# Identity products around a transpose, a scaling on VectorE, and later weight and query loads in a fused DeltaNet and maxout-FFN kernel

## The chip, the cores and the metric

The kernel runs on one core of one Trainium2 chip. The metric is device time in microseconds of one execution, and a kernel's time is the median of its runs. A core has five engines with queues of their own: PE (TensorE, matrix products), DVE (VectorE), ACT (ScalarE), POOL (GpSimd) and SP (SyncE, which only issues DMAs here). Each engine works its queue in program order, so an instruction that waits holds up all that stand behind it on its engine. PEld is the loading of PE's stationary operand.

## The reference

Queries, keys and values are 4 batches x 8 heads x 768 positions x 48. The first layer is a delta rule with a 48x48 state for each batch and head; the second is a maxout FFN over 3072 tokens of width 384, with hidden width 768.

```python
k_n = k / (np.linalg.norm(k, axis=-1, keepdims=True) + 1e-06)
for t in range(S):
    y[:, :, t] = einsum('bhd,bhde->bhe', q[:, :, t], state)
    v_old = einsum('bhde,bhd->bhe', state, k_n[:, :, t])
    state = state + beta[t] * einsum('bhd,bhe->bhde', k_n[:, :, t], v[:, :, t] - v_old)
x = y.transpose(0, 2, 1, 3).reshape(B * S, H * D)
h = maximum(maximum(x @ w1, x @ w2), x @ w3)
out = h @ w_out
```

## The kernel before, in words

**Chunks.** The 768 positions are cut into 12 chunks of 64. Two chunks make a group of 512 tokens, so there are six groups. Inside a chunk the recurrence is written with products: of keys with keys (the tile `at`), of keys with queries (`pt`), and with the inverse of a triangular matrix (`ut`), which is found by `solve(m)` for a whole group at once. `solve` is a generator: each `yield` is one elimination step, two VectorE operations (L561 and L565), and the main program takes steps with `some(solving, n)`. Group 0 is solved before the FFN starts, group 1 while the FFN of group 0 runs.

**One chunk's links.** For chunk c: `halves_z` (e) and `halves_u` (f) finish the second half of the inverse for chunk 1 (products p_e, p_f); `join_z` (z, p_z) and `join_u` (j, p_j) join the halves; `turn_t1` (d) transposes; `old_k` (k) subtracts p_k from v on VectorE at L755; `old_q` (q) is p_q; `new` (u) is p_u; `step` (s) adds p_s to the state `st` on VectorE at L801; `to_y` (y) is p_y; `to_x` (x) transposes y on PE (p_x, L832) and copies it to `xt` on ACT (L839). The FFN of the group reads `xt`.

**Other letters.** S is one solve step, M masks `pt`, T n is `turn(n, (1,))`, the transposes of query unit n with their copy, after which `load_q(n + 3)` is issued while n + 3 < 11; P is the product of keys and queries of a unit. A unit is half a chunk's batches: chunk c has the units 2c and 2c + 1. Query units take turns in three buffers (`qall`), values (`v_t`) in three.

**The FFN of group 0** (`ffn(0)`) yields after each hidden tile: i = 0, 1, 2 are the three maxout weights of the first 128 hidden columns for 256 tokens, and so on to i = 17; from i = 18 on they are 512 tokens wide; i = 27 to 30 are the outputs. Each of them is three products p_h (L1224; two records each) into one of two PSUM buffers, and a copy on ACT or a maximum on VectorE (L1238). The loop over i in the main program (L1452) writes out by hand what stands between two such tiles: the strings in `FIRST` (links, solve steps, turns), `EARLY_LINKS` (links of chunks 2 and 3), loads, fetches and conversions. The order of the text is the order on each engine.

**Weights.** The weights come as 24 pieces of 384 KB. `fetch(queue)` issues the DMA of the next one into one of five buffers (`w_bits`), and waits on its queue until that buffer is free. `some(conv, 1)` converts one piece: three ACT operations (L247 to L249), a VectorE shift (L259) and a GpSimd addition (L263), the last two one conversion late. Pieces 0 to 5 are fetched before the loop; pieces 9 to 17 are used from i = 18 on. The first four conversions stand before the loop, six at i = 0 to 5, and the rest from i = 11 on.

**Values.** `load_v(c)` issues two DMAs, and `scale(c, nrm)` (L295) multiplies the chunk's values by the norms of its keys, on GpSimd for chunks 0 to 9 and on VectorE after that. `prep_values(2)` is the scaling of chunk 2, at i = 8.

**Around the change.** The end of the part before the loop is, in the order of the text: the products p_u and p_y of chunk 0, the transposes of `halves_t(1)`, the start of `solve(1)` (norms, ACT's zeroing of its PSUM tile y_p at L525, L547), `to_x(0)`, one conversion. Then the loop starts with i = 0. `busy(n, of)` (L1290) issues n products of the identity with `of` into a PSUM tile p_w of the same two buffers as p_h; nothing reads it. It is called once before the change, with six products, at the very start.

Of the kernel before, what the change touches and what calls it, by code (L numbers as in the profile page):

```python
# [23 lines left out]
def kernel(  # L24
# [31 lines left out]
    nc = tc.nc  # L56
# [32 lines left out]
    def ps_ffn(shape, name):  # L89
        return psum.tile(shape, FP32, name=name, tag="ffn", bufs=2)  # L90

    def ps_two(name):
        return pairs.tile([128, 2, 512], FP32, name=name, tag="two", bufs=3)
# [7 lines left out]
    ident = const.tile([128, 128], FP32, name="ident")  # L101
# [16 lines left out]
    def rows(bb):  # L118
        return slice(C * bb, C * (bb + 1))
# [6 lines left out]
    def load(src, dst, n, queues):  # L126
        c, g = divmod(n, 2)
        for bb in range(2):
            queues[bb].dma_start(
                out=dst[rows(bb ^ g), :, 0:D],  # L130
                in_=src[2 * bb + g, :, c * C : (c + 1) * C, :].rearrange(
                    "h p d -> p h d"
                ),
            )
# [4 lines left out]
    def load_k(n, queues=one_queue):  # L139
        load(k, kpad[place(n)], n, queues)  # L140

    def load_q(n, queues=one_queue):
        load(q, qpad[n % NQ], n, queues)

    def load_v(c, queue=nc.sync):
        vts[c] = work.tile([128, 2, H, D], FP32, name="v_t", bufs=3)
        for bb in range(2):
            queue.dma_start(  # L148
                out=vts[c][rows(bb)].rearrange("p g h d -> p (g h) d"),
                in_=v[2 * bb : 2 * bb + 2, :, c * C : (c + 1) * C, :].rearrange(  # L150
                    "b h p d -> p (b h) d"
                ),
            )
# [66 lines left out]
    def fetch(queue=nc.scalar):  # L220
        if fetched[0] < len(pieces):
            _, src, (a, b) = pieces[fetched[0]]
            st = work.tile([128, 2 * 384], U32, name="w_bits", bufs=5)
            queue.dma_start(
                out=st.rearrange("p (a b) -> p a b", a=a), in_=src
            )
            staged.append(st)
            fetched[0] += 1
# [63 lines left out]
                )  # L292
            nrms[2 * m + cc] = t[:, 16:32].rearrange("p (g h) -> p g h", g=2)

    def scale(c, nrm):  # L295
        (nc.vector if c > 9 else nc.gpsimd).tensor_tensor(
            out=vts[c], in0=vts[c],
            in1=nrm[:, :, :, None].to_broadcast([128, 2, H, D]), op=ALU.mult,
        )

    def prep_values(c):

        if c in nrms:
            scale(c, nrms.pop(c))


    nrm_0 = const.tile([128, 2, 2, H], FP32, name="nrm_0")
# [179 lines left out]
    def blocks(m, queue=nc.sync):  # L487
        if m == 1:
            xs[m] = in_wo(0)
        else:  # L490
            xs[m] = work.tile([128, 2, HB * BL + HB], FP32, name="x_bl", bufs=1)
        queue.dma_start(
            out=in_rows(xs[m]),
            in_=at_d[m].rearrange("c f b h j i -> (c f b h) j i"),
        )
# [323 lines left out]
    def to_x(c):  # L819
        m, cc = divmod(c, 2)  # L820
        if m not in xts:
            xts[m] = work.tile([128, KT, TOK], FP32, name="xt")
        y_f = yts.pop(c).rearrange("p g h d -> p g (h d)")
        xt = xts[m][:, :, cc * 256 : (cc + 1) * 256].rearrange(
            "p t (g x) -> p g t x", g=2
        )
        p_x = ps_two("p_x")
        for g in range(2):
            if g and not c:
                p_x = ps_two("p_x")  # L830
            for t in range(KT):
                nc.tensor.transpose(  # L832
                    p_x[:, g, t * 128 : (t + 1) * 128],
                    y_f[:, g, t::KT],
                    ident,
                )
            of = p_x[:, :, 0 : KT * 128].rearrange("p g (t x) -> p g t x", t=KT)
            if not c:
                nc.scalar.copy(xt[:, g], of[:, g])  # L839
        if c:  # L840
            nc.scalar.copy(xt, of)
# [37 lines left out]
    def less_first(f):  # L879
        part = (slice(None), slice(None), slice(f * 128, (f + 1) * 128))  # L880
        for i in (1, 2):
            nc.vector.tensor_tensor(
                out=w_sb[i][part], in0=w_sb[i][part], in1=w_sb[0][part],
                op=ALU.subtract,
            )

    def turn_first(fs):
        p_f = ps_two("p_t")
        for i, f in enumerate(fs):
            for t in range(KT):  # L890
                nc.tensor.transpose(
                    p_f[:, i, t * 128 : (t + 1) * 128],
                    w_sb[0][:, t, f * 128 : (f + 1) * 128],
                    ident,
                )
        for i, f in enumerate(fs):
            nc.scalar.copy(
                w_sb[0][:, :, f * 128 : (f + 1) * 128],
                p_f[:, i, 0 : KT * 128].rearrange("p (t x) -> p t x", t=KT),
            )  # L900
# [375 lines left out]
    def some(gen, n):  # L1276
        for _ in range(n):
            if next(gen, gen) is gen:
                break
# [10 lines left out]
    def busy(n, of):  # L1290
        p_w = ps_ffn([128, TOK], "p_w")[:, 0 : of.shape[1]]
        for _ in range(n):
            nc.tensor.matmul(p_w, ident, of)
# [55 lines left out]
    some(conv, 1)  # L1349
    placed(1, 0)  # L1350
    scale(0, nrm_0[:, 0])
    placed(1, 1, nc.gpsimd.tensor_copy)
    blocks(1, nc.gpsimd)
    for _ in range(2):
# [16 lines left out]
    halves_t(1)  # L1371
    solving = solve(1)
    some(solving, 1)
    to_x(0)
    some(conv, 1)


# [28 lines left out]


    FIRST = {
        0: "e1 s0 S1 S1", 1: "f1 k1 S1 S1 S1", 2: "z1 d1 M2 S1 S1",
        3: "j1 S1 q1 M3 S1 S1", 4: "u1 T4", 5: "y1", 6: "s1 T5", 7: "x1 T6",  # L1410
        8: "T7", 14: "P4", 15: "P5", 21: "P6", 22: "P7",
    }

# [12 lines left out]
    def links(m, names):  # L1426
        for name in names.split():
            f, i = name[0], int(name[1])
            if f in RECURS and m < GROUPS:
                RECURS[f](2 * m + i)  # L1430
            elif f in MADE and m + 1 < GROUPS:
                MADE[f](2 * (m + 1) + i)
            elif f in UNIT and m + 1 < GROUPS:
                UNIT[f](4 * (m + 1) + i)
            elif f == "N" and m + 2 < GROUPS:
                load_blocks(4 * (m + 2) + i)

    def queries(names):
        for name in names.split():
            f, n = name[0], int(name[1])  # L1440
            if f not in OF_KEYS:
                links(0, name)
                continue
            OF_KEYS[f](n)
            if f == "T" and n + 3 < 11:
                load_q(n + 3)
# [3 lines left out]
    CONVERTED = {*range(6), *range(11, 25)}  # L1450
    FETCHED = {8: 1, 12: 1, 13: 1, 14: 1, 18: 2, 19: 2, 20: 1, 21: 1}
    for i, _ in enumerate(ffn(0)):  # L1452
        if i < 7:
            fetch(nc.sync if i else nc.gpsimd)
        if i == 0:
            scale(1, nrm_0[:, 1])
        if i == 1:
            load_q(4)
            load_q(5)
        if i == 2:  # L1460
            load_q(6)
        for _ in range(FETCHED.get(i, 0)):
            fetch(nc.gpsimd)
        if i == 25:
            some(conv, 1)
        if i == 21:
            some(solving, 3)
        queries(FIRST.get(i, ""))
        links(1, EARLY_LINKS.get(i, ""))
        if i == 20:  # L1470
            solving = solve(2)
            some(solving, 1)
        if i in CONVERTED:
            some(conv, 1)
        if i == 0:
            fetch(nc.gpsimd)
        if 3 < i < 14:
            some(solving, (3, 2, 2, 2, 3, 3, 3, 3, 2, 2)[i - 4])
        if i in (8, 13):
            prep_values(i // 4)  # L1480
        if i in (4, 8):
            for n in range(2):
                load_k(8 + 2 * (i > 4) + n, (nc.gpsimd, nc.gpsimd))
        if i == 11:
            load_q(11, (nc.gpsimd, nc.gpsimd))
        if i in (3, 9, 10, 21):
            load_v((3, 9, 10, 21).index(i) + 2)
        if i == 18:
            blocks(2)
        if i == 23:  # L1490
            prep_values(4)
        if i > 21:
            some(solving, (3, 1, 2, 2, 3, 5, 5, 5, 5)[i - 22])
        if i in (27, 28, 29):
            load_blocks(i - 15, nc.sync)
        if i in (15, 17, 19, 22, 25, 27):
            less_first((15, 17, 19, 22, 25, 27).index(i))
        if 27 <= i < 30:
            turn_first((2 * (i - 27), 2 * (i - 27) + 1))
# [55 lines left out]
```

## Time and profile before

| | us |
|---|---|
| median of 3 runs | 508.12 |
| the runs | 510.18, 508.12, 507.56 |
| the profiled execution | 506.9 |
| its span, first to last instruction | 505.2 |
| PE busy | 484.0 (96%) |
| DVE busy | 361.1 (71%) |
| POOL busy | 187.1 (37%) |
| ACT busy | 169.4 (34%) |
| mean granted PE clock | 0.968 |

All times inside the kernel count from the span's start. The profile's page cuts the span into 40 slices of 12.6 us and gives the busy tenths of each engine in each, and under PEclk the share of full speed that PE's clock was granted. A table by stretches gives for any stretch the busy us of the five engines, with the number of their instructions in brackets, then that clock, the share of the DMA engines and GB/s. A timeline row has the start, the length, the engine, the line, the operation with what it writes and reads, its size and how often, and in square brackets the idle time before it and what ended that. A row of waits has who waited for whom, the total, the number of waits and the longest, in us. A product of 32-bit data shows as two records on PE, a transpose as one.

### The profile page before, as it was taken

The numbers are of one execution on the slowest core, as the hardware profiler recorded it, in microseconds if no ns is written. First come the engines' busy times: TensorE is split into PE (matmuls) and PEld (weight loads), VectorE is DVE, ScalarE is ACT, GpSimd is POOL, SyncE is SP. The second block draws the span as 40 slices with busy tenths as digits, with TensorE's granted clock in tenths as the row PEclk, the third lists the DMA queues.
The fourth block names the chain that finished last, engine by engine and source line by source line (L and its number), as shares of the span: only waits on it lengthen the run. The fifth ranks groups of instructions, "written<-read, shape, count | busy, mean of one in ns | idle before, by whom it ended". The sixth has DMA issues, their size and how long they took to land.

```text
span 505.2 us, 18676 instructions
## 1 busy us (share of the span) xinstructions
PE 484.0 (96%) x8064; PEld 338.0 (67%) x8064; DVE 361.1 (71%) x835; ACT 169.4 (34%) x320; POOL 187.1 (37%) x311
## 2 busy tenths in 40 slices
PE   7678989999999999999999999999999999999996
PEld 6467767855566555565565565555797457998895
DVE  5888799787996441799652999565998874468753
ACT  5585664885422142210152200242201032212210
POOL 7434472793391935770395880501000020000000
PEclk9855899999999999999999999999999999999999
DMA  8937869864045934544584652744224230340002
GB/s 114 205 50 214 195 142 160 198 181 137 3 120 134 191 72 77 146 119 117 112 156 104 158 137 74 149 72 96 64 54 90 47 86 15 85 94 1 0 18 47
DMA packets 109121, 53.50 MB, mean 106 GB/s; under 512 B 92208, under 2 KB 102864, under 8 KB 109040
## 3 DMA queue, kind: packets, MB, share of 16 engines
q1 hardware_dynamic: 97280, 31.78, 31.0%
q0 software_dynamic: 9216, 19.85, 16.5%
q8 instruction: 63, 1.03, 0.9%
q10 hardware_dynamic: 2544, 0.69, 0.8%
q14 instruction: 18, 0.15, 0.1%
HBM read 39.17 MB, written 13.11 MB: 103 GB/s over the span
## 4 chain that ended last, share of the span: by engine, by line
PE 76%; DVE 11%; ACT 4%; DMA 3%; SPq 3%; issue 2%; POOL 0%; DVEq 0%; ACTq 0%; POOLq 0%
PE p_h L1224 28%; PE p_o L985 13%; PE p_o L1262 12%; PE p_c L1163 5%; DVE tmp L561 3%; PE p_g L415 2%; PE p_m L905 2%; PE p_u L771 2%; PE p_k L743 2%; DVE y_p L565 2%; DMA kmore<-in_k_dram 2%; PE p_y L813 2%; PE p_s L794 2%; PE p_q L743 1%; PE p_j L726 1%
## 5 line engine op out<-in xcount | busy, mean ns | idle before, releaser
L1224 PE MATMUL p_h<-xt,w_sb 128*128 128x512 f32 (+1 forms) x450 | 186.8, 558 | 0.6 <-ACT xt L839 0.6
L1224 PEld LDWEIGHTS p_h<-xt,w_sb 128*128 128x128 f32 x450 | 82.4, 193 | 69.2 <-issue 61.6
L1238 DVE TENSOR_TENSOR h<-h,p_h 128x512 f32<-128x512 f32 (+1 forms) x42 | 25.5, 607 | 46.8 <-PE p_h L1224 46.3
L565 DVE TENSOR_TENSOR y_bl<-y_bl,tmp 128x31 f32<-128x31 f32 (+20 forms) x139 | 50.4, 363 | 4.8
L561 DVE TENSOR_TENSOR tmp<-x_bl,y_bl 128x31 f32<-128x31 f32 (+20 forms) x139 | 48.8, 351 | 3.9
L1262 PE MATMUL p_o<-wo_sb,h 128*128 128x384 f32 x144 | 48.9, 490 | 0.0
L373 POOL DMA_DIRECT2D turned<-in_q_dram x72 | 39.3, 554 | 4.6 <-POOL turned L368 3.1
L1262 PEld LDWEIGHTS p_o<-wo_sb,h 128*128 128x128 f32 x144 | 26.7, 190 | 17.2
L1234 ACT ACTIVATE h<-p_h 128x512 f32<-128x512 f32 x24 | 14.3, 597 | 69.2 <-PE p_h L1224 69.2
L263 POOL TENSOR_TENSOR w_sb<-mant,up 128x384 int32<-128x384 int32 x18 | 19.0, 1054 | 39.5 <-DVE mant L259 37.8
L415 PEld LDWEIGHTS p_g<-kqt 48*64 48x64 f32 x1216 | 24.5, 142 | 9.2 <-issue 6.3
L415 PE MATMUL p_g<-kqt 48*64 48x64 f32 (+1 forms) x1216 | 27.7, 241 | 0.9 <-ACT kqt L344 0.8
L1268 ACT COPY o_sb<-p_o 128x384 f32<-128x384 f32 x12 | 5.8, 479 | 62.6 <-PE p_o L1262 56.5
L801 DVE TENSOR_TENSOR st<-st,p_s 48x768 f32<-48x768 f32 (+1 forms) x18 | 17.1, 949 | 12.7 <-PE p_s L794 12.4
L399 DVE TENSOR_TENSOR pt<-p_g,mask 128x512 f32<-128x512 f32 x20 | 13.8, 690 | 17.0 <-PE p_g L415 16.9
L598 POOL DMA_DIRECT2D ut<-y_d x4 | 2.6, 653 | 60.6 <-DMA y_d<-y_bl 60.6
L148 POOL DMA_DIRECT2D v_t<-in_v_dram x14 | 11.6, 832 | 35.3 <-PE p_u L771 35.3
L368 POOL MEMSET turned<- 128x96 f32 x18 | 3.3, 191 | 49.4 <-DVE kqt L389 49.4
L771 PEld LDWEIGHTS p_u<-v_t,ut 64*64 64x64 f32 x768 | 13.5, 141 | 8.4 <-issue 7.3
L432 ACT COPY at<-p_g 128x512 f32<-128x512 f32 x22 | 12.8, 585 | 17.4 <-DVE pt L399 15.4
L373 POOL DMA_DIRECT2D turned<-in_k_dram x32 | 17.5, 556 | 1.2 <-POOL turned L368 1.2
L1163 PE MATMUL p_c<-xt,w_sb 128*128 128x256 f32 x72 | 17.7, 379 | 0.0
(239 smaller groups left out, 907.3 us busy)
## 6 DMA issues: line engine op xcount, KB each, us to landing
w_bits<-in_moe_w_dram SPq DMA_DIRECT2D x9, 384.0 KB, 6.2
w_bits<-in_moe_w_dram POOLq DMA_DIRECT2D x9, 384.0 KB, 5.7
turned<-in_q_dram POOLq DMA_DIRECT2D x72, 48.0 KB, 2.8
out_dram<-o_sb SPq DMA_DIRECT2D x36, 96.0 KB, 2.3
y_x<-y SPq DMA_DIRECT2D x32, 96.0 KB, 3.0
qall<-y_x SPq DMA_DIRECT2D x32, 96.0 KB, 2.8
v_t<-in_v_dram POOLq DMA_DIRECT2D x14, 192.0 KB, 5.0
at_d<-at SPq DMA_DIRECT2D x72, 32.0 KB, 3.0
```

What stands on the lines that cost most here:

```text
L263: nc.gpsimd.tensor_tensor(out=dst.bitcast(I32), in0=mant_v.bitcast(I32), in1=up_v, op=ALU.add)
L373: (queue, nc.gpsimd)[i].dma_start(out=t[p0 : p0 + 32, bb, at : at + NP * 2 * D].rearrange("p (j x) -> p j x", j=NP), in_=(k, q)[i][2 * bb ...
L415: nc.tensor.matmul(p_g[rows(bb ^ (g * i)), par, c0 : c0 + C * (1 + whole)], kq[:, 0], kq if whole else kq[:, i],)
L561: nc.vector.tensor_tensor(out=t_v, in0=row.to_broadcast(t_v.shape), in1=column.to_broadcast(t_v.shape), op=ALU.mult,)
L565: nc.vector.tensor_tensor(out=rest, in0=rest, in1=t_v, op=ALU.subtract)
L771: nc.tensor.matmul(p_v[rows(bb ^ g), g, i], ut[c % NU][rows(bb), g, h], rhs[rows(bb), g, h],)
L801: nc.vector.tensor_tensor(out=s_v[r], in0=s_v[r], in1=p_s[r, :, 0 : H * D], op=ALU.add)
L985: nc.tensor.matmul(to[:, g], a[j][:, 128 * g : 128 * (g + 1)], b[j], start=(start and g == j == 0), stop=(stop and g == 1 and j == len(a) ...
L1163: nc.tensor.matmul(to, w[stays], moves, start=(n == 0), stop=(n == len(terms) - 1))
L1224: nc.tensor.matmul(p_h, w_sb[i][:, t, f * 128 : (f + 1) * 128], xt[:, t, lo : lo + w], start=(t == 0), stop=(t == KT - 1),)
L1238: nc.vector.tensor_tensor(out=h, in0=h, in1=p_h, op=ALU.max)
L1262: nc.tensor.matmul(p_o, stays, moves, start=(n == 0), stop=(n == len(terms) - 1))
```

## The change

It does six things to the stretch from p_y of chunk 0 to i = 10:

- Two products of the identity stand before `to_x(0)` and one after it. Nothing reads them.
- The scaling of chunk 1 (at i = 0) is on VectorE instead of GpSimd.
- Two solve steps of group 1 go from i = 0 and i = 1 to i = 2.
- T4 goes from i = 4 to i = 5, and the load of query unit 7 with it.
- The fetches of i = 3 to 6 go to i = 7 to 10, on the same queue (SP).
- The loads of query units 4, 5, 6 stand at i = 1, 3, 4 instead of 1, 1, 2; the load of chunk 2's values stands at i = 5 instead of 3.

```diff
-    def scale(c, nrm):
-        (nc.vector if c > 9 else nc.gpsimd).tensor_tensor(
+    def scale(c, nrm, engine=None):
+        (engine or (nc.vector if c > 9 else nc.gpsimd)).tensor_tensor(
...
     some(solving, 1)
+    busy(2, ident)
     to_x(0)
+    busy(1, ident)
     some(conv, 1)
...
     FIRST = {
-        0: "e1 s0 S1 S1", 1: "f1 k1 S1 S1 S1", 2: "z1 d1 M2 S1 S1",
-        3: "j1 S1 q1 M3 S1 S1", 4: "u1 T4", 5: "y1", 6: "s1 T5", 7: "x1 T6",
+        0: "e1 s0 S1", 1: "f1 k1 S1 S1", 2: "z1 d1 M2 S1 S1 S1 S1",
+        3: "j1 S1 q1 M3 S1 S1", 4: "u1", 5: "y1 T4", 6: "s1 T5", 7: "x1 T6",
         8: "T7", 14: "P4", 15: "P5", 21: "P6", 22: "P7",
     }
...
     for i, _ in enumerate(ffn(0)):
-        if i < 7:
+        if i < 3 or 6 < i < 11:
             fetch(nc.sync if i else nc.gpsimd)
         if i == 0:
-            scale(1, nrm_0[:, 1])
-        if i == 1:
-            load_q(4)
-            load_q(5)
-        if i == 2:
-            load_q(6)
+            scale(1, nrm_0[:, 1], nc.vector)
+        if i in (1, 3, 4):
+            load_q((1, 3, 4).index(i) + 4)
...
-        if i in (3, 9, 10, 21):
-            load_v((3, 9, 10, 21).index(i) + 2)
+        if i in (5, 9, 10, 21):
+            load_v((5, 9, 10, 21).index(i) + 2)
```

## The prediction

> **What bounds the kernel now.** I read the page's 40 slices first, for the engine that is never idle and for the clock.
>
> ```profile
> PE   7678989999999999999999999999999999999996
> DVE  5888799787996441799652999565998874468753
> PEclk9855899999999999999999999999999999999999
> ```
>
> A slice is 12.6 us. From the eighth on (about 90 us) PE is full, and only slices two to five show a low granted clock. A table of busy times by stretches says the first exactly:
>
> ```profile
> 92.00:500.00 408.00, 407.85 (x6297) 274.22 (x6295) 285.34 (x648) 113.33 (x209) 141.14 (x238) 1.00 0.42 95
> ```
>
> Columns: PE, PEld, DVE, ACT, POOL busy, clock, DMA share, GB/s. PE is busy 407.85 of 408 us. So the end is set by how soon PE gets past the first 92 us, and a microsecond won there is kept if nothing later starts to wait. All edits lie at 35 to 90 us.
>
> Tenth-of-a-microsecond stretches place the clock's changes at 18.96 (down), 22.38 (up), 25.79 (down) and 53.09 (up): 3.41 us apart, or eight times that. The same table, cut on that grid, shows what each window held:
>
> ```profile
> 18.96:22.38 3.42, 3.42 (x56) 2.64 (x60) 3.03 (x11) 1.53 (x3) 2.27 (x5) 0.50 1.35 224
> ...
> 39.44:42.85 3.41, 2.64 (x93) 2.50 (x89) 2.55 (x6) 3.31 (x7) 1.76 (x3) 0.50 0.93 332
> 42.85:46.27 3.42, 2.85 (x9) 2.27 (x10) 3.15 (x9) 2.36 (x5) 2.18 (x3) 0.50 0.71 191
> 46.27:49.68 3.41, 3.41 (x76) 2.58 (x78) 3.10 (x10) 0.41 (x2) 0.00 (x0) 0.50 0.89 197
> 49.68:53.09 3.41, 3.41 (x72) 3.05 (x65) 1.48 (x5) 2.14 (x4) 3.19 (x3) 0.50 0.84 149
> 53.09:56.51 3.42, 3.42 (x135) 2.93 (x135) 1.50 (x4) 1.54 (x5) 1.74 (x2) 1.00 0.85 234
> ```
>
> The clock rises after a window that PE filled (3.42 of 3.42, and the one ending at 53.09), not after one with 0.57 us idle (42.85), and not after 46.27:49.68, which is full but more than half p_e. The timeline of PE names the work:
>
> ```profile
> 42.83 1.52 PE L832 MATMUL p_x<-ident,y 128*128 128x128 f32 x6 [0.77 <-ACT y_p L525]
> 44.92 2.93 PE L1224 MATMUL p_h<-xt,w_sb 128*128 128x256 f32 x6 [0.57 <-ACT xt L839]
> 47.77 1.93 PE L685 MATMUL p_e<-ut,at 64*64 64x32 f32 x64
> 49.50 1.94 PE L794 MATMUL p_s<-u,kpad 64*64 64x48 f32 x64
> 51.37 2.40 PE L1224 MATMUL p_h<-xt,w_sb 128*128 128x256 f32 x6
> 53.70 1.14 PE L696 MATMUL p_f<-z,t 64*64 64x32 f32 x64
> 54.65 1.13 PE L743 MATMUL p_k<-st,kqt 48*64 48x48 f32 x64
> ```
>
> Two idle spots, 0.77 and 0.57 us, stand around the transposes p_x; all until 53.09 runs at half speed. Who pays: VectorE's waits at 41 to 56.5 us, then PE's at 41 to 92 us (total, times, longest):
>
> ```profile
> DVE st L801 <- PE p_s L794: 1.9, 1, 1.9
> DVE v_t L755 <- PE p_k L743: 1.6, 1, 1.6
> DVE y L817 <- PE p_y L813: 0.3, 1, 0.3
> DVE h L1238 <- PE p_h L1224: 0.3, 1, 0.3
> ```
> ```profile
> PE p_t L338 <- DMA qall<-in_q_dram: 1.0, 1, 1.0
> PE p_u L771 <- issue: 1.0, 1, 1.0
> PE p_x L832 <- ACT y_p L525: 0.8, 1, 0.8
> PE p_x L832 <- DVE st L801: 0.7, 1, 0.7
> ```
>
> After 56 us VectorE is the tighter engine (busy 16.72 of 17.50 us at 56.5 to 74, PE 15.43): it runs solve(1)'s steps.
>
> **The change, part by part.** *Three products.* The six products at the start (12 records, L1293) run from 2.01 to the next work at 4.73: 0.45 us each, at half clock by their neighbours (four transposes take 0.89 there, 0.63 from 6.02, 1.01 in the slow stretch at 18.86). Two of them are 0.91 us from p_y's end at 42.06, so p_x starts at 42.97 instead of 42.83: +0.14 us. The third fits after p_x, into the 0.57 us, and leaves some 0.2 us idle. Their tile p_w takes turns with p_h's two PSUM buffers, but nothing reads it, so no copy holds it up. If the clock doesn't react, the cost is 0 to +0.14 us.
>
> *Clock.* Window 42.85:46.27 then holds products, transposes and p_h, with 0.2 us idle. The highest idle time that was followed by a rise is 0.11 us (the grid run back gives a window from 1.90 to 5.31; PE starts at 2.01); the 0.57 us in 42.85:46.27 itself were not. 0.2 is nearer to 0.11, so I take a rise at 46.27. Window 39.44:42.85 is also filled, but 2.6 us of it are 64x48 products; a rise at 42.85 is possible, not assumed. From 46.27 to 53.09 PE worked 6.82 us at half clock; at full clock that is 3.41 us. Bounds of PE's lead: 0 and 3.41 + (46.27-42.85)/2 = 5.1 us.
>
> [...]
>
> *What VectorE lets through.* VectorE's own work (solve(1)'s start, L547 and L259) ends at 49.62 whatever PE does. With PE ahead, p_e would end at 47.9, p_s at 49.0, p_f at 51.2. VectorE's three waits in 49.62 to 55.91 (1.89, 0.31, 1.61) are 3.81 us; they are the most that can go.
>
> *Scaling of chunk 1 on VectorE.* The same line on VectorE for chunks 10 and 11 takes 0.95 us, on GpSimd 1.47 to 1.57. Its input v was asked for at 43.35 and 44.20 and landed 4.8 to 6.4 us later, about 49.7: it holds VectorE 0.1 us at the most. The price is 0.95 + 0.1 = 1.05 us on VectorE, and st (L801), queued behind it, starts at 50.7 instead of 51.51. Now the scaling is hidden in GpSimd (51.48 to 52.98, old_k needs it at 55.91). With the lead p_k would end at 52.6, so there it would come 0.4 us late. At the old clock it lies in the 1.89 us wait and costs nothing.
>
> *Solve steps.* One step leaves i=0, one leaves i=1, two come at i=2; VectorE's sum to there is the same. They put the st and v_t operations ahead of about 0.4 to 1.2 us of steps. Worth 0 by itself, since VectorE has no wait between them.
>
> Sum on VectorE at i=2: 3.81 - 1.05 = 2.76 us gained. PE's lead of 3.4 us minus 0.14 covers it, so VectorE's number holds.
>
> *DMA.* Fetches of i=3 to 6 (issued at 58.07, 61.62, 68.67, 69.34) go to i=7 to 10, each 384 KB, 6.2 us to landing. Their users convert at i=11 and after (87.44 on), cover some 10 us. v of chunk 2 goes from 58.68 to behind q7, which puts it near 67; 5.7 us later is about 73, where GpSimd's scaling stood at 73.55; old_k(2) comes at 80.69: cover 5 us. k10 and k11 are queued behind that scaling on GpSimd; they are used at i=13 and 15. q5 and q6 go an i or two later, with 8 us and more until T5 and T6. T4 moves one i back: its copy on ACT is 0.59 us and its first reader is old_q(2) at i=9, some 10 us later; q7 is issued behind it and read by T7 at 76.82, 10 us after its issue at 66.75 now. Each is 0 while the cover holds.
>
> The place without cover is q9: PE already waits 1.01 us for it at 85.84. SP issues it behind T6 at 75.71 and 76.75 and it takes 7.3 to 8.7 us. After the change v2, one fetch and q8 lie right ahead of it on SP's queue instead of q8 behind two older fetches, and one more follows. Bounds: -1.0 (the wait goes) to +6.2 (a whole fetch more). I take +0.4, near the row that exists, since the load in front of q9 is exchanged rather than added.
>
> **Sum:** -2.76 + 0.4 = -2.4 us on the profiled execution, 506.9 (span 505.2 and 1.7 around it): 504.5. The three timed runs are 507.56, 508.12 and 510.18, all above it. From the profiled one to the highest is 3.3 us, as much as one clock window; I read part of this as a clock that rises later in them, which the change would also take away. Subtracting 2.4 from the median gives 505.7; I take 505.1, between the two.
>
> **The rivals.** *As above*, clock up by about 47: 503.4 to 506.3, chance 0.64.
>
> *The clock doesn't rise earlier* (the change doesn't do what it says): 0.2 us of idle, or the 64x48 products beside it, spoil each window. Then VectorE's waits stay, the scaling hides in them, +0.14: 506.9 to 508.4. For it: 46.27:49.68 was full and did nothing. Against it: 49.68:53.09 held 1.7 us of 64x48 work and did. Chance 0.13.
>
> [...] Chance 0.05. [...]
>
> *q9 takes the gain back.* PE's wait at t1 (i=11) grows by 1.5 to 3 us: 506.3 to 508.5, chance 0.11. For it: DMA share is 1.04 at 74 to 92 against 0.70 at 56.5 to 74, so work goes from the freer stretch to the fuller. Against: v2 and one fetch fall in 66 to 72, where SP had issued only q7 and two fetches.
>
> *Slower by the same place:* q9 lands a whole fetch later, 6.2 us, and PE stands for it: 6.2 - 2.76 = +3.4, 511.5. It decides once q9 takes more than 8.7 + 2.8 = 11.5 us. Chance 0.07.
>
> **Numbers.** The forecast is 505.1. The range of 503.4 to 508.5 leaves out the slower case and the tails. Half a per cent, 2.5 us, is about what a measurement of this kernel can tell from no change: faster than that is below 505.6. Some three quarters of the first case lie there, and little else: 0.50; slower 0.07; the rest, 0.43, within.
>
> **What would show it.** The clock's rise at 43 to 47 instead of 53; p_x 0.1 us later; st at 50.7, right behind a 0.95 us scaling; no VectorE wait at v_t; p_k from about 51.6; the copy L569, now at 88.53, at about 85.8; PE's wait at q9 within 1 us of 1.01. It is wrong if the rise stays at 53, if PE waits more than 3 us at 82 to 90, or if PE, now ahead, idles so much at 50 to 56 that the clock falls again (it fell after windows with 2.14 and 0.87 us of work).

## The result, and the profile after

The changed kernel takes 515.08 us (median of six runs, 512.98 to 517.84); the kernel before, run beside it, 508.14 (507.56 to 510.18). The ratio is 1.0136, with a 95% interval of 1.0096 to 1.0176. It is slower by 7 us, and the time is outside the range that was given. The profiled execution took 515.15 us, its span 513.4. Two executions, one of e_wide_b at 807.89 us (granted clock 0.557) and one of a_fetch_back at 514.72, were in a slower state and are left out of the ratios below.

From the page of the kernel after: busy tenths of PE and VectorE and the granted clock in 40 slices, here of 12.8 us.

```profile
PE   7779799969999999999999999999999999999996
DVE  5898897846999351499762799654998874478752
PEclk9657999979999999999999999999999999999999
```

Two things differ from before. The low clock at the start is over after four slices instead of five, as forecast. And the ninth slice (103 to 115 us) has a 6 in PE's row and a 7 in the clock's, where PE was full before: a new hole, well behind the edits.

The table by stretches of the kernel after, cut on its clock grid (columns as in the prediction); the first row belongs to the edits, the others to the hole and to what follows it:

```profile
41.48:44.89 3.41, 3.41 (x41) 3.22 (x36) 2.99 (x5) 2.13 (x5) 3.37 (x4) 0.50 0.64 196
...
106.33:109.74 3.41, 0.97 (x64) 0.78 (x64) 1.94 (x5) 1.55 (x4) 3.40 (x6) 1.00 0.92 160
109.74:113.15 3.41, 2.20 (x66) 1.65 (x67) 1.04 (x3) 1.73 (x4) 2.07 (x4) 0.50 0.98 267
...
117.00:510.00 393.00, 391.14 (x5905) 262.77 (x5904) 271.93 (x626) 97.90 (x180) 125.28 (x217) 1.00 0.39 88
```

In the hole PE works 0.97 of 3.41 us, then the clock stands at 0.50 for two windows (to 116.57), and from 117 us on PE is full again (its work ends at 508.5, and it is idle for 0.33 us before that). So whatever is lost by 117 us is lost at the end. PE's timeline there, with the wait in square brackets:

```profile
107.52 0.25 PE L713 MATMUL p_z<-ut,at 32*32 32x32 f32 x4 [2.12 <-DMA ut<-y_d]
...
110.95 1.19 PE L713 MATMUL p_z<-ut,at 32*32 32x32 f32 x64 [2.08 <-DMA ut<-y_d]
112.07 5.06 PE L1224 MATMUL p_h<-xt,w_sb 128*128 128x512 f32 x6
117.06 0.75 PE L726 MATMUL p_j<-z,t 32*32 32x32 f32 x64
```

The same stretch before:

```profile
104.92 1.35 PE L713 MATMUL p_z<-ut,at 32*32 32x32 f32 x128
106.19 2.84 PE L1224 MATMUL p_h<-xt,w_sb 128*128 128x512 f32 x6
108.97 0.75 PE L726 MATMUL p_j<-z,t 32*32 32x32 f32 x64
```

There p_z had no wait. The difference at p_j, 8.1 us, is: three waits for `ut`, 4.6 us (one of 0.39 is left out here); p_h at half clock, 2.2; p_z in pieces and half of it at half clock, 0.8; and 0.5 by which PE came late to p_z. `ut` is the inverse of group 1, which `solve(1)` stores (L586, `y_d`) and reads back (L598) through DRAM. The solve is hardly late: its last copy (L569) stands at 89.59, before at 88.53. SP's issues tell where the rest arises. The kernel after (start, time for the issue, line, destination and source):

```profile
83.00 0.56 SPq L224 DMA_DIRECT2D w_bits<-in_moe_w_dram  x1
...
85.77 4.81 SPq L224 DMA_DIRECT2D w_bits<-in_moe_w_dram  x1
...
93.00 6.03 SPq L445 DMA_DIRECT2D at_d<-at  x4
99.13 1.68 SPq L586 DMA_DIRECT2D y_d<-wo_sb  x2
104.25 4.05 SPq L598 DMA_DIRECT2D ut<-y_d  x8
```

The kernel before:

```profile
90.47 1.80 SPq L445 DMA_DIRECT2D at_d<-at  x4
92.37 1.15 SPq L586 DMA_DIRECT2D y_d<-wo_sb  x2
96.85 5.00 SPq L598 DMA_DIRECT2D ut<-y_d  x8
```

The last late fetch takes 4.81 us to issue where the one before it took 0.56; the four stores of `at` take 6.03 instead of 1.80; the store of `y_d` starts at 99.13 instead of 92.37 and the reload at 104.25 instead of 96.85.

### The profile page after: what moved, and what is told of

It is laid out like the page before. It is cut to its first block, busy times and chain, and to the rows that moved or that the text cites. A ratio compares the mean times of both kernels' runs of the same rounds, so it can differ in the third digit from the quotient of the medians.

```text
span 513.4 us, 18690 instructions
## 1 busy us (share of the span) xinstructions
PE 489.3 (95%) x8070; PEld 341.6 (67%) x8070; DVE 362.1 (71%) x836; ACT 169.3 (33%) x320; POOL 186.2 (36%) x310
## 3 DMA queue, kind: packets, MB, share of 16 engines
q8 instruction: 63, 1.03, 0.9%
## 4 chain that ended last, share of the span: by engine, by line
PE 83%; DMA 6%; ACT 3%; issue 2%; SPq 2%; DVE 2%; POOL 0%; POOLq 0%; ACTq 0%
PE p_h L1224 32%; PE p_o L985 12%; PE p_o L1262 12%; PE p_c L1163 5%; PE p_u L771 3%; PE p_g L415 3%; PE p_y L813 3%; PE p_m L905 2%; PE p_k L743 2%; PE p_q L743 2%; PE p_j L726 2%; DMA kmore<-in_k_dram 2%; PE p_s L794 2%; SPq L129 2%; PE p_z L713 1%
## 5 line engine op out<-in xcount | busy, mean ns | idle before, releaser
L561 DVE TENSOR_TENSOR tmp<-x_bl,y_bl 128x31 f32<-128x31 f32 (+20 forms) x139 | 50.7, 365 | 3.9
L565 DVE TENSOR_TENSOR y_bl<-y_bl,tmp 128x31 f32<-128x31 f32 (+20 forms) x139 | 48.5, 349 | 4.8
L415 PEld LDWEIGHTS p_g<-kqt 48*64 48x64 f32 x1216 | 25.6, 146 | 10.5 <-issue 6.9
L415 PE MATMUL p_g<-kqt 48*64 48x64 f32 (+1 forms) x1216 | 29.1, 246 | 1.5 <-ACT kqt L344 0.8
L598 POOL DMA_DIRECT2D ut<-y_d x4 | 2.6, 653 | 60.2 <-DMA y_d<-y_bl 60.2
L432 ACT COPY at<-p_g 128x512 f32<-128x512 f32 x22 | 12.8, 587 | 18.4 <-DVE pt L399 16.1
L755 DVE TENSOR_TENSOR v_t<-v_t,p_k 128x768 f32<-128x768 f32 x11 | 10.5, 951 | 11.5 <-PE p_k L743 9.7
```

The source lines that it names most:

```text
L415: nc.tensor.matmul(p_g[rows(bb ^ (g * i)), par, c0 : c0 + C * (1 + whole)], kq[:, 0], kq if whole else kq[:, i],)
L561: nc.vector.tensor_tensor(out=t_v, in0=row.to_broadcast(t_v.shape), in1=column.to_broadcast(t_v.shape), op=ALU.mult,)
L565: nc.vector.tensor_tensor(out=rest, in0=rest, in1=t_v, op=ALU.subtract)
```

## The experiments

Each kernel ran beside the kernel before on the same chip, and the ratio is to that kernel. It is worked out from the single runs, so it can differ a little from the quotient of the medians.

### Which edit loses the time

Two theories went on record first: A, that the late fetches hold up SP's queue ahead of the store of `y_d`; B, that the loss is in the later values and queries (GpSimd waits 7.5 us for chunk 2's values after the change). Two kernels undo parts of the change, the first the fetches alone, the second fetches, loads and T4.

a_fetch_back:

```diff
-        if i < 3 or 6 < i < 11:
+        if i < 7:
```

> The changed kernel with its four fetches put back from i=7 to 10 to i=3 to 6; all else stays changed. Theory A (SP's queue): the four fetches stand on SP ahead of the last values load and of the store of pt's partner at_d (L445) and of solve(1)'s result (L586), whose issue went from 92.37 to 99.13 us; PE then waits 4.6 us for ut at p_z and its clock falls. By A the store is back near 92 to 93, PE's wait at p_z is gone, and the time is 507 to 509.5. Theory B (the values and query loads): chunk 2's values, which GpSimd now awaits for 7.5 us, and T4's later place hold the chain up; then this kernel stays at 512 to 516.

509.22 us against 508.3, 1.003 (0.9994 to 1.0066). The loss is gone, and PE has no wait for `ut` at all.

a_loads_back, the same and:

```diff
-        3: "j1 S1 q1 M3 S1 S1", 4: "u1", 5: "y1 T4", 6: "s1 T5", 7: "x1 T6",
+        3: "j1 S1 q1 M3 S1 S1", 4: "u1 T4", 5: "y1", 6: "s1 T5", 7: "x1 T6",
...
-        if i in (5, 9, 10, 21):
+        if i in (3, 9, 10, 21):
```

with the query loads at i = 1, 1, 2 again.

> The changed kernel with the fetches, the query loads, T4 and chunk 2's values all back in their old places; the three products, the scaling on VectorE and the solve steps stay changed. Theory A: about as the kernel with only the fetches back, 506 to 509. Theory B: this one is the first to come back, 506 to 509, while the other is above 512. By my prediction's own account of PE and VectorE it would be 505.4 (2.8 us won); by theory C (PE stands still at places inside a row of products, 3.8 us in all, which takes the clock's gain away) it is 507 to 508.5.

509.38 us, 1.0023 (0.9995 to 1.0052), the same as a_fetch_back. Theory B falls: the later loads are worth nothing that can be measured. (Theory C is explained further down.)

Two kernels do one part alone, starting from the kernel before. b_fetch_late moves the four fetches (the first diff the other way round):

> The kernel before, with only the four fetches moved from i=3 to 6 to i=7 to 10. Theory A: the store of solve(1)'s result is issued 5 us and more later than 92.37 and the time is 511 to 516. Theory B: 507.5 to 509, since the converted pieces are due only from i=11 on.

515.8 us in four runs, 1.0151 (1.0095 to 1.0206): the whole loss from the four fetches alone. The profile is of its fastest execution, 511.76 us; it shows 2.5 us of PE's waits for `ut` and a p_h of 4.74 us behind them.

b_products adds the three products only:

```diff
+    busy(2, ident)
     to_x(0)
+    busy(1, ident)
```

> The kernel before, with only the three products around p_x. The clock's rise comes at 43 to 48 us instead of 53. Theory C: the gain at 45 to 53 us is lost again in stops inside rows of products; 507 to 508.5, with two or three stops of 0.7 to 2 us that the profile puts down to issue. By my prediction's account the scaling on GpSimd ends 0.4 us late and the time is 505.5 to 506.5.

507.93 us, 0.9995 (0.997 to 1.0019). The part that was to bring the gain brings none, though its clock rises at 44.2 us.

### Queue order or bytes

In d_pool_fetch the late fetches are issued from GpSimd's queue, so SP's queue is free of them:

```diff
-            fetch(nc.sync if i else nc.gpsimd)
+            fetch(nc.sync if 0 < i < 3 else nc.gpsimd)
```

> The changed kernel with its late fetches (i=7 to 10) issued from GpSimd's queue instead of SP's; the DMAs move the same bytes at the same places of the program. Theory A (they stand on SP's queue ahead of the store of solve(1)'s result): SP stores at 92 to 95 us again, PE waits under 1 us for ut, 507 to 510.5. Theory D (the DMA engines themselves are overloaded at 75 to 100 us, whoever issues): 512 to 516 as the changed kernel.

514.92 us in four runs, 1.0146 (1.0115 to 1.0177). The loss stays. SP's issues in d_pool_fetch:

```profile
83.28 10.45 SPq L148 DMA_DIRECT2D v_t<-in_v_dram  x4
...
99.51 2.09 SPq L586 DMA_DIRECT2D y_d<-wo_sb  x2
```

No fetch stands in this queue, and SP's other issues stall just the same: the loads of `v_t` take 10.45 us (5.71 before), and the store of `y_d` is as late as in the kernel after. Theory A, the order of the queue, falls. Theory D replaces it: by it the fetches' bytes delay the store (99.51 us here, 92.37 before), whichever queue they come from. Under D the issues may stay late if the bytes go early. d_split does that: at i = 3 to 6 it fetches 112 of the 128 partitions of a piece, and at i = 7 to 10 the other 16, all from SP:

```diff
+            nc.sync.dma_start(out=to[0:112], in_=src[0:112])
...
+        nc.sync.dma_start(out=to[112:128], in_=src[112:128])
...
-        if i < 3 or 6 < i < 11:
+        if i < 3:
             fetch(nc.sync if i else nc.gpsimd)
+        elif i < 7:
+            most()
+        elif i < 11:
+            rest()
```

> The changed kernel, with each of its four late fetches cut in two: 112 of the 128 partitions come at the old place (i=3 to 6), the last 16 at the new one (i=7 to 10), both from SP. SP still issues four DMAs at the new places ahead of the store of solve(1)'s result, but they carry an eighth of the bytes. Theory D (bytes that the DMA engines must move at 75 to 100 us): SP's store is back at 92 to 95 us, 507.5 to 510. Theory A2 (four more DMAs to issue there, whatever their size): 512 to 516.

509.69 us, 1.0023 (0.9996 to 1.005). The loss is gone with four late issues still in the queue. (The split is by partitions, so this run doesn't tell bytes from packets.) Its SP (the helper shifts the lines by 16, so L461 is the store of `at`, L602 that of `y_d`):

```profile
90.86 2.96 SPq L461 DMA_DIRECT2D at_d<-at  x4
93.93 1.15 SPq L602 DMA_DIRECT2D y_d<-wo_sb  x2
```

d_two leaves only the fetches of i = 9 and 10 late:

```diff
-        if i < 3 or 6 < i < 11:
+        if i < 5 or 8 < i < 11:
```

> The changed kernel with two of the four late fetches (those of i=3 and 4) back in their places, and the two others late (i=9 and 10). Theory D: about half of the bytes are gone from the full stretch, but those that stay are the last ones, right ahead of the store: 509 to 513. If only the last of them matters: 513 to 516.

510.29 us, 1.0057 (1.0028 to 1.0085): 2.9 us, somewhat under half the loss of four.

The table by stretches puts these kernels in order. Its last column, GB/s, over the 18 us from 74 to 92:

| kernel | GB/s, 74 to 92 | MB in 18 us | reload of ut issued at | PE waits for ut, us | ratio |
|---|---|---|---|---|---|
| before | 155 | 2.8 | 96.85 | 0 | 1 |
| d_split | 167 | 3.0 | 99.83 | 1.1 | 1.0023 |
| a_fetch_back | 168 | 3.0 | 99.61 | 0 | 1.003 |
| d_two | 175 | 3.2 | 100.98 | 2.4 | 1.0057 |
| after | 186 | 3.3 | 104.25 | 4.6 | 1.0136 |
| b_fetch_late | 204 | 3.7 | 101.96 | 2.5 | 1.0151 |
| d_pool_fetch | 209 | 3.8 | 104.06 | 3.1 | 1.0146 |

The share of busy DMA engines doesn't sort them: it is 1.17 in a_fetch_back, which shows no wait, and 1.15 after. GB/s parts those that lose from those that don't, but only among these kernels. In the same stretch f_wide_alone and c_tiny32, two kernels of the next sections with every fetch in its old place, move 175 and 187 GB/s, and neither waits for `ut`. So what is shown is that these four transfers cost time when they come late, from either queue, and not when 7/8 of each goes early; a limit in GB/s is not shown.

How much the round trip had to spare is read from the time between the reload's issue and PE's arrival at p_z: 8.1 us before. PE waits for nothing in the kernels with 5.9 us or more (a_fetch_back has 6.3), and waits in all with less (b_products with 5.87 for 0.7 us, d_split with 5.1 for 1.1). About 2 us were to spare.

### Where the gain of the earlier clock went

In the kernels with the three products the clock rises at 42.6 to 48.7 us instead of 53.1, and mostly no time is won. PE's timeline of the kernel after shows stops that the profile calls "issue", that is, PE waits for nothing that is recorded:

```profile
50.72 0.81 PE L1224 MATMUL p_h<-xt,w_sb 128*128 128x256 f32 x3 [1.07 <-issue]
...
52.41 1.13 PE L743 MATMUL p_k<-st,kqt 48*64 48x48 f32 x61
54.27 0.32 PE L743 MATMUL p_k<-st,kqt 48*64 48x48 f32 x3 [0.73 <-issue]
...
61.00 0.34 PE L726 MATMUL p_j<-z,t 32*32 32x32 f32 x17 [1.98 <-issue]
```

They fall in the middle of p_h, p_k and p_j. Counted from PE's first record they come before numbers 977, 1105 and about 1231: 128 apart, give or take what the count misses. Theory C is that PE stops at fixed record numbers whatever stands there. The rival is that the stops belong to these products or to the low clock before them. Two kernels keep the three products and save the six records at the start, so that all later work moves back to its old numbers; a third moves it by 64.

c_three_a (on a_loads_back) and c_three_b (on b_products):

```diff
-    busy(6, ident)
+    busy(3, ident)
```

> The changed kernel with all loads and fetches in their old places, and three identity products fewer at the very start, so that the number of PE's products ahead of each later one is that of the kernel before. Theory C2: PE stops before a fixed record number (977, 1105, 1231, 1358 in four kernels, 128 apart), whatever product stands there, because its instructions come in blocks; the six added records moved the stop at 1105 from p_h into p_k, whose end VectorE waits for. By C2 the stop is in p_h again, VectorE has its v_t 1 to 2 us sooner, and the time is 505 to 507.5. Theory C3: the stops belong to those products (their data or semaphores); then they stay in p_k and the time is 508 to 510, as with six.

508.77 us, 1.0032 (1.0012 to 1.0052). The stop at 977 lies in p_f here, where it was in p_h.

> The kernel before with the three products around p_x added and three taken away at the very start: as many records as before. By C2 the stop at record 1105 leaves p_k: 505.5 to 507.5. By C3 as with the three products alone: 507 to 509.

508.16 us, 1.0008 (0.9986 to 1.003). The stop at 1105 lies in p_h, after the end of p_k, and VectorE no longer waits for p_k. With the same record numbers b_fetch_late, which has none of the products, stops in p_h too, for 1.9 us. So the stops went where C2 puts them, and neither time came down as C2 forecast. PE reached p_e of chunk 0 at 32.4 and 32.9 us here, and at 32.8 and 30.4 in a_loads_back and b_products: the start differs from profile to profile by more than was to be won.

c_tiny32 adds 64 records of almost no work to a_loads_back, ahead of p_e of chunk 0:

```diff
+    def tiny(n):
+        p_w = ps_ffn([128, TOK], "p_w")
+        for i in range(n):
+            r = slice(32 * (i % 4), 32 * (i % 4) + 32)
+            nc.tensor.matmul(p_w[r, 0:1], ident[r, r], ident[r, r][:, 0:1])
```

> The changed kernel with all loads and fetches in their old places and 32 products of 32x32 by one column (64 records) added ahead of chunk 0's p_e, where PE waits 2.2 us for ACT. By C2 the stops stay at record numbers 977, 1105, 1233 and 1361 counted with the added ones, so in the program they fall 64 records earlier: in p_s, p_f, p_z and p_q instead of p_h, p_k, p_j and p_u; the time within 2 us of 509. By C3 they stay in p_h, p_k, p_j and p_u.

514.54 us in two runs against 507.23, 1.0137 (1.009 to 1.0183), where a_loads_back is at 1.0023; the expectation had 507 to 511. Yet the 64 records take only 1.03 us, at 29.04, and PE still waits 1.24 us for the copy of `ut` after them. PE's waits from 41 to 92 us in c_tiny32 (total, times, longest):

```profile
PE p_q L743 <- issue: 2.7, 1, 2.7
PE p_z L713 <- issue: 1.6, 1, 1.6
PE p_f L696 <- issue: 1.1, 1, 1.1
```

The stops have moved to other products, and there they stand at records 1105, 1232 and 1359: at the old numbers. One product on the list of the expectation, p_s, had none. The stops don't explain the whole time: PE is 2.7 us behind the kernel before at the p_h of 116.96 us, and the other 3.8 us of the longer span come after it. The page has a row that fits, in the kernel after as before:

```profile
q8 instruction: 63, 1.03, 0.9%
```

63 packets of 16 KB; 63 x 128 = 8064, and the kernel before has 8064 records on PE, the one after 8070. c_tiny32 has 8134 records and 64 packets. So about one packet for each 128 records fits these counts. With the loads of weights and the semaphore instructions counted, the stops stand behind 1985, 2242 and 2498 instructions of PE in the kernel after and behind 2754 in the one before, give or take one, which is 256 or 257 apart.

The trace has the time of each packet. In the kernel after, packets of this queue end at 49.10, 52.84 and 59.46 us, and PE goes on after its three stops at 50.72, 54.27 and 61.00, 1.4 to 1.6 us later. In the kernel before one ends at 64.38, and PE goes on in p_u at 65.65, 1.3 us later. The profiles of the 17 kernels (e_wide_b by its second run) have 36 stops of 0.5 us or more between 40 and 92 us that are put down to issue. All stand at these places, and each ends 1.3 to 1.7 us after such a packet. What PE waits for there no row says, and the ground that theory C2 gives, instructions that come in blocks, is not shown. Why PE stops at some of these places and not at others (three times between 40 and 92 us in the kernel after, once in the one before) stays open. A full clock is not needed for it: the longest stop, 2.7 us in c_tiny32, comes after PE had run at half clock from 59.56 us on.

A stop can stand in front of a reader. In the kernel after the one at 1105 has moved into p_k, for which VectorE's v_t waits 1.91 us. VectorE's timeline of the kernel after:

```profile
50.59 0.95 DVE L801 TENSOR_TENSOR st<-st,p_s 128x768 f32<-128x768 f32 x1
...
54.62 0.95 DVE L755 TENSOR_TENSOR v_t<-v_t,p_k 128x768 f32<-128x768 f32 x1 [1.91 <-PE p_k L743]
```

### Old record numbers with the same start

The kernels e_wide keep the work of the start (2.93 us on PE from 2.00 in e_wide_b2, 2.93 from 2.01 before) and spend half the records on it: three products of 256 columns in place of six of 128, so that p_k has its old numbers.

```diff
-    busy(6, ident)
+    wide(3)
...
+            nc.tensor.matmul(
+                p_w.rearrange("p (a b) -> p a b", a=2), ident,
+                ident[:, None, :].to_broadcast([128, 2, 128]),
+            )
```

e_wide_a is a_loads_back with it:

> The changed kernel with all loads and fetches in their old places, and the six products at the very start written as three of twice the width: the same PE time there, six records fewer, so that each later product has the record number that it has in the kernel before. Theory C2: no stop in p_k, VectorE 1 to 2 us earlier, and the start is not slowed as with three narrow products: 505.5 to 507.5. If the stops did not cost the gain: 508 to 509.5, as with six narrow ones.

508.2 us, 0.9995 (0.9974 to 1.0016): no gain.

e_wide_b is b_products with it:

> The kernel before with the three products around p_x, and three of twice the width at the very start instead of six: as many records as before. By C2 505 to 507; otherwise 507 to 508.5, as with the three products alone.

506.57 us against 507.76, 0.9967 (0.9945 to 0.9988): faster than the kernel before. It was run again:

> The same kernel again: the kernel before, the three products around p_x, and three of twice the width at the very start instead of six. Theory C2: 505 to 507, a ratio of 0.995 to 0.999; no stop inside p_k, VectorE's v_t (L755) 2 us earlier after the start of chunk 0's p_e than in the kernel before (25.8 us).

506.49 us against 508.22, 0.9977 (0.9947 to 1.0006). Its PE timeline:

```profile
54.20 1.16 PE L743 MATMUL p_k<-st,kqt 48*64 48x48 f32 x64
...
57.57 0.92 PE L1224 MATMUL p_h<-xt,w_sb 128*128 128x256 f32 x3 [1.36 <-issue]
```

p_k runs in one piece, the stop follows in p_h, and VectorE does not wait for p_k. By the ratios the gain is 0.33 and 0.23 per cent, 1.2 to 1.7 us, and the second interval just takes in 1. It is the fastest version that was run. That the missing wait makes this gain is not shown: c_three_b has p_k in one piece too, its st and v_t stand at 52.25 and 56.17 us against 52.34 and 56.27 in e_wide_b2, its p_e of chunk 0 starts at the same 32.9, and its time is that of the kernel before.

Is it the wide start by itself? f_wide_alone is the kernel before with nothing but that:

> The kernel before with only the start's six products written as three of twice the width: six PE records fewer, no products around p_x. If the gain is that of the earlier clock with the blocks of instructions in their old places, this one has neither and stays within 0.3% of the kernel before (its stops move by six records the other way). If fewer records alone make the gain, 505 to 507.

508.94 us, 1.0011 (0.9978 to 1.0043): no.

Do the moved solve steps help? f_wide_steps is e_wide_b with them:

> As e_wide_b2, with the solve steps of the change as well (two go from i=0 and 1 to i=2), but not its scaling on VectorE. They put VectorE's v_t 0.4 to 1.2 us ahead of steps, and VectorE works without a wait behind it: 505 to 507, the same as e_wide_b2 within 0.3%. If the steps are what takes the gain from the kernel with scaling and steps, 507.5 to 508.5.

507.92 us, 0.998 (0.9955 to 1.0004): by the ratio no difference from e_wide_b2 that can be told, though the median lies where the steps were to be the loss. Its VectorE waits 1.6 us at v_t for the scaling on GpSimd, which ends too late for the earlier p_k: the prediction had put this at 0.4 us, and it is a wait that the scaling on GpSimd can bring. From e_wide_a (0.9995) this kernel differs by the scaling alone. f_scale_alone is the kernel before with the scaling only:

```diff
-            scale(1, nrm_0[:, 1])
+            scale(1, nrm_0[:, 1], nc.vector)
```

> The kernel before with only chunk 1's scaling on VectorE. By my prediction it lies in VectorE's 1.9 us wait for p_s and costs nothing: 507 to 508.5. If VectorE stands behind it for the landing of chunk 1's values, in runs in which the clock is up early, 508 to 510.

508.77 us, 0.9996 (0.9962 to 1.003). By itself it costs nothing. But its waits from 44 to 60 us show what it does:

```profile
DVE v_t L296 <- DMA v_t<-in_v_dram: 0.8, 1, 0.8
...
PE p_k L743 <- DVE st L801: 2.0, 1, 2.0
```

The scaling waits 0.8 us for chunk 1's values at the head of VectorE's queue, st stands behind it, and PE stands 2.0 us for st. In e_wide_a the two waits are 0.6 and 1.5 us; in e_wide_b2 there is neither. That the scaling takes e_wide_a's gain is read from these waits; the ratios of e_wide_a and f_wide_steps, 0.15 per cent apart with intervals that overlap, agree but don't prove it. e_wide_a also waits 1.0 us for `ut` at p_z, which e_wide_b2 does not.

## Why the prediction was wrong, step by step

**DMA: this step failed, and it decides the sign.** The step asked for each moved fetch who reads the piece, found 10 us of cover, and put "0 while the cover holds". The cover held: no conversion waits for a fetched piece. What it didn't ask is who else needs the DMA engines at 84 to 104 us. It had the row that should have warned (share 1.04 at 74 to 92 us), and used it only for q9. Four fetches of 384 KB, 1.5 MB, went into a stretch that moved 2.8 MB in 18 us (3.3 MB after the change, so not all of it was moved there). They delay the store and reload of `ut` by 7 us, of which about 2 had cover, and PE, which had been full there, loses 8.1 us in the profile. b_fetch_late alone gives the +7.5; d_pool_fetch and d_split show that it is neither SP's order nor the number of issues, but the late transfers themselves.

**Chunk 2's values, 0 while 5 us of cover hold: failed, at little cost.** They were to be issued near 67 and to land at about 73; they were issued at 71.11, and GpSimd's scaling stood 7.46 us for them, to 80.22 (73.55 before). VectorE then waits 1.74 us for GpSimd at v_t of chunk 2 (81.73; before 80.69, no wait), which is most of what turns its 0.8 us of lead into 1.1 of delay. In a_fetch_back the same wait is 0.35 us, though GpSimd waits 6.08 us there too, and a_loads_back, which has the loads at the old place, is no faster.

**q9: wrong place.** The rival that ended slower had the right kind of cause, a transfer made late by fetches, and PE's wait at the wrong transfer. PE's wait for q9, 1.0 us before, is gone in the kernel after. The mechanism's size, 6.2 us for one fetch more, was not tested.

**Three products and the clock: right.** The rise is at 44.89 us instead of 53.09. (The grid lies 1.4 us off that of the profile before, so the window that counts is another.) The window 41.48:44.89, shown above, is full (3.41 of 3.41), the transposes p_x hold 1.49 us of it, and a rise follows. For the chance of 0.05 no run shows a ground: the clock rose after this window, and in the kernel before after 18.96:22.38, of which eight transposes hold some 1.9 us. The window 58.54:61.96 holds 1.44 us of work, the 1.98 us stop being the rest, and the clock falls to 0.50 after it, from 61.96 to 65.37, as the last sentence of the prediction feared, though 10 us later. Not every early rise is the change's: f_scale_alone and b_fetch_late have no products and rose at 45.1 and 45.0 us. So an early rise comes without the products too, and that of one profile is in part luck.

**What VectorE lets through, -2.76 us: mis-sized.** st came at 50.59, forecast 50.7, right behind a scaling of 0.96 us (49.72): this part holds to a tenth. v_t was to follow at 53.15 without a wait; it came at 54.62 after 1.91 us for p_k. So the gain on VectorE was 1.3 us, and the other 1.5 are two of PE's stops: p_k began at 52.41 instead of 51.6, behind the 1.07 us in p_h, and stood for 0.73 us itself. The profile of before had such a stop too (p_u, 1.0 us, among the waits shown), and I passed over it. Part of the 1.3 is only order, since the two moved solve steps now come after v_t: at the same step, the one of 207 elements, VectorE is 0.8 us ahead (63.64 for 64.42). And the solve's last copy, forecast for 85.8, came at 89.59, later than before.

**Scaling on VectorE, 1.05 us: price right, effect missed.** Held against GpSimd's time it looked cheap. Its cost is what stands behind it: up to 2.0 us of waiting on PE at p_k. f_scale_alone has that wait and is no slower, so how much of it reaches the end is not shown.

**Solve steps, 0: right** within what f_wide_steps against e_wide_b2 can tell.

**"A microsecond won there is kept": too strong.** a_loads_back reaches p_z 2.1 us sooner than before, counted from p_e of chunk 0, and ends 0.1 us sooner. About 1.0 us goes in a wait of p_u for v_t at 130 us and some 0.4 us in a longer stop at 264 us; the rest I didn't find. b_products shows it more plainly: it reaches p_z 1.2 us before the kernel before, then waits 0.7 us there for `ut` and 0.7 at p_u for v_t, and is 0.3 us behind at 153 us. Its solve's last copy stands at 88.46, against 88.53: PE had its lead, and VectorE, which makes `ut`, had none. And p_e of chunk 0 itself starts at 30.1 to 31.3 us where the clock first rises by 8 us, and at 32.4 to 33.0 where it first rises at 14 to 18, so that a lead counted from it is good to a microsecond or two. What lifts e_wide_b by 1 to 2 us therefore stays open.

Left open: why 1.5 MB more make single issues take 4.8 us, and what PE waits for at its stops.

## What to carry to other kernels

A DMA that is moved needs two covers: the reader of its own data, and every other transfer in the stretch that receives it, above all a round trip through DRAM that a full PE waits for (4.6 us here). A higher granted clock is worth only what the engine's waits leave of it (in b_products it rose at 44.2 us instead of 53.1, at a ratio of 0.9995), so look for rows of "issue" and for the engine that reads PE's result before counting half-clock time as a gain. And an operation moved to an idle engine is priced by what queues behind it while it waits for its input, not by its own length (in f_scale_alone 2.0 us of PE's waiting, behind a scaling that waits 0.8 us).

## What the runs showed of the hardware

- Where PE stops for "issue", the places lie 256 or 257 of its own instructions apart (128 records with their loads of weights), whatever product stands there: 36 stops of 0.5 to 2.7 us in 17 kernels, each ending 1.3 to 1.7 us after a packet of 16 KB on the queue "instruction". 64 more records ahead of them moved the stops to other products, and that kernel was 7.3 us slower than the one before; its stops from 41 to 92 us add up to 5.4 us, against 1.0 in the kernel before.
- A DMA issue on SP that took 0.56 us took 4.81 us 2.8 us later in the same kernel, and when the added fetches came from GpSimd's queue instead, the loads of `v_t` in that queue took 10.45 us to issue, against 5.71 before.
- 2.4 to 4.6 us of waiting on PE cost it up to 3.0 us more at half clock: p_h of 128x512 took 4.5 to 5.06 us there, and 2.84 at full clock.
- Half-clock time at small products cost little: the mean granted clock (median of the runs) was 0.968 before and 0.973 to 0.976 in b_products, a_loads_back and a_fetch_back, 5 to 8 us less at half clock by 2 x span x the difference, at no gain in time.
